# Second expert layer: block sums and statistics on other engines, the activation of later pairs after a reload

## The chip, the cores and the metric

One core of one Trainium2 chip runs the whole program in one launch. The metric is device time in microseconds (us) of that launch, the median of several runs. The engines are PE (TensorE, matrix products; PEld are its weight loads), DVE (VectorE), ACT (ScalarE), POOL (GpSimd) and SP (SyncE, which here issues DMAs). Each runs its own instructions in the order in which they were issued; between engines semaphores make them wait.

## The reference

```python
def reference(**kwargs):                      # cut
    attn_out = _attn_ref(**attn_kwargs)       # 4 batches, 12 heads, 448 tokens, heads mixed before and after the softmax
    x = attn_out.transpose(0, 2, 1, 3).reshape(1792, 768)
    x = _moe_ref(x=x, **moe_kwargs)           # 768 -> 2048 -> 768, a gated activation between
    return _moe2_ref(x=x, **moe2_kwargs)

def _moe2_ref(x, w_in, w_out, g_ln):          # 768 -> 1024 -> 768
    h = x @ w_in
    e = np.exp(h - np.max(h, axis=-1, keepdims=True))
    sm = e / (np.sum(e, axis=-1, keepdims=True) + 1e-09)
    solu = h * sm
    mu = np.mean(solu, axis=-1, keepdims=True)
    var = np.mean((solu - mu) ** 2, axis=-1, keepdims=True)
    ln = (solu - mu) / np.sqrt(var + 1e-06) * g_ln
    return ln @ w_out
```

The change is in `_moe2_ref`, the second expert layer.

## The kernel before

The program has four stages, one after the other: attention, the first expert layer, and the two matrix products of the second expert layer, here called **phase 1** (`h = x @ w_in`) and **phase 2** (`ln @ w_out`). All products keep float32 precision by splitting each operand into a rounded part and a rest: three matmuls stand for one (lines 1167 to 1169).

In the second layer the 1792 tokens are 14 tiles `t` of 128, worked on as 7 **pairs** `p`. For each pair the 2 by 2 blocks of the left matrix (two tiles of tokens by two halves of the inner dimension) and of the weights are multiplied in seven block products instead of eight (`SEVEN`; `product` and `keep_` in `seven`). Such a scheme needs sums of blocks on the left, S1 to S4 (`s_sum`, line 1086, in phase 1; `l_sum`, line 1121, in phase 2), sums of weight blocks (`prep1`, `prep2`, lines 948 to 951), and additions of the products (`part_copy` on ACT, line 1181; `part_add` on DVE, line 1184). Some products may start only when an earlier addition has released or filled their PSUM bank.

Phase 1 works through one pair like this. The left blocks and sums are split by ACT (`x2_h`, line 1092) and DVE (`x2_l`, line 1095). PE makes seven products of 9 matmuls. ACT and DVE collect them into two tiles `h` of 128x1024. For each tile DVE takes the maximum (`h2_max`, 1235), ACT the exponential with its sum (`h2_exp`, 1239), POOL and DVE make the reciprocal (1242, 1245), DVE multiplies `h`, `e` and the reciprocal in place over `e` (`h2_solu`, 1248), and SP stores the result to a DRAM scratch `xl2` (`h2_store`, 1253). For pairs below `EARLY` (2) the layer norm's mean and variance are made at once (`stat`, 1141 and 1142, on DVE; `rstd`, 1146 to 1148, on POOL).

Phase 2 loads a tile back (`el_load`, 1103), makes the statistics of pairs from `EARLY` on, normalizes on ACT (`el_ln`, 1152), transposes on PE (`tr`, 1108), copies from PSUM (`lf_copy`, 1115), makes the block sums (1121), splits (`l_h` on ACT, 1132; `l_l` on DVE, 1135) and makes seven products of 12 matmuls. While phase 1 ends, the 28 pieces of `w_out` are loaded (`w_load`, 1044) into the buffers that the last products of phase 1 leave, and split (`w_h` on ACT, 1047; `w_l`, 1051, odd pieces on POOL, even ones on DVE).

Buffers: `h2` has 5 tiles, `wout` (which holds `e`) 3, `s` (block sums) 4, `ot` (outputs) 3. The order of every engine's instructions is made when the program is built: `Order` takes tasks with a duration and a priority given in the code (`add(engine, duration, priority, function, ...)`, smaller goes first) and lists them in a simulated time; the engines then run them in that order. A changed engine or duration can thus move the instructions around it.

Of the kernel before, what the change touches and what calls it, by code (L numbers as in the profile page):

```python
# [7 lines left out]
F32 = mybir.dt.float32  # L8
# [649 lines left out]
def moe(nc, od, pl, c1, c2, last_x, r_sr, r_psa, r_psb, near, xs, c_near, c_in2, c_out2, c_t1, c_t2, c_o2, xl2, w_in, w_out, w_in2, w_out2, g_ln, ident_in, out):  # L658
    add = od.add
# [7 lines left out]
    def open1():  # L667
        pl.open([(n, b, 'right', SB) for n, b in (('wout', 3), ('win', 3), ('t', 2), ('raw', 2), ('m', 2), ('v', 1))])
        keep['half'] = pl['v'].tile([128, 1], F32, tag="half", name="half")
        keep['ebias'] = pl['v'].tile([128, 1], F32, tag="ebias", name="ebias")  # L670
        nc.gpsimd.memset(keep['half'], 0.5)
        nc.gpsimd.memset(keep['ebias'], -896.0 * 2**23)
# [332 lines left out]
    def close_o():  # L1005
        pl.close(['g', 'psb'])
        pl.open([('h2', 5, 'left', SB), ('st2', 3, 'left', SB), ('st3', 4, 'left', SB), ('pw', 4, 'left', PSUM)])
# [10 lines left out]
    ring.update({n: od.ring(b) for n, b in dict(st3=4, s=4, ot=3, h2=5, pstr=4).items()})  # L1018
# [55 lines left out]
    sx, ht, et, st, lnp, ott, elt, lf = ({} for _ in range(8))  # L1074
# [23 lines left out]
    EL = ('h2', 'h2', 'h2', 'wout')  # L1098

    def el_load(t):  # L1100
        n = EL[t % 4]
        elt[t] = pl[n].tile([128, 1536 if n == 'wout' else FF2], F32, tag=n, name="el")[:, :FF2]
        nc.sync.dma_start(out=elt[t], in_=xl2[:, t])

    def tr(t, i):
        ps = pl['pstr'].tile([128, 4, 128], F32, tag="pstr", name="ps_tr")
        for j in range(4):
            nc.tensor.transpose(ps[:, j], elt[t][:, i * 512 + j * 128:i * 512 + (j + 1) * 128], keep['ident'])  # L1108
        lnp[t, i] = ps
# [27 lines left out]
    def stat(t, late):  # L1137
        if late:
            st[t] = pl['st3'].tile([128, 32], F32, tag="st3", name="st3")
# [4 lines left out]
    def rstd(t):  # L1144
        s, r = st.pop(t), keep['ls'][:, 2 * t:2 * t + 2]
        nc.gpsimd.tensor_scalar(s[:, 6:7], s[:, 5:6], 1e-6, 1.0, op0=ALU.add, op1=ALU.mult)
        nc.gpsimd.tensor_tensor(out=r[:, 0:1], in0=s[:, 6:7], in1=keep['mh'], op=ALU.pow)
        nc.gpsimd.tensor_scalar(r[:, 1:2], s[:, 4:5], r[:, 0:1], -1.0, op0=ALU.mult, op1=ALU.mult)
# [21 lines left out]

    def out_tile(ph, t):
        d = ht if ph == 0 else ott
        if t not in d:
            d[t] = pl[('h2', 'ot')[ph]].tile([128, (FF2, DM)[ph]], F32, tag=('h2', 'ot')[ph], name=('h2', 'ot')[ph])
        return d[t].rearrange("p (i n) -> p i n", i=2)
# [10 lines left out]
    def seven(ph, p, pr, ldeps, wdeps, r_left):  # L1186
        n = (512, 384)[ph]
        mm, dur, bank, m = ring['pw'], (9 * 227, 12 * 174)[ph], {}, []
        rg = ring[('h2', 'ot')[ph]]
        own = len(rg.users)  # L1190
# [42 lines left out]
    def h2_max(t):  # L1233
        st[t] = pl['st2'].tile([128, 32], F32, tag="st2", name="st2")
        nc.vector.tensor_reduce(st[t][:, 0:1], ht[t], axis=AX.X, op=ALU.max, negate=True)  # L1235

    def h2_exp(t):
        et[t] = pl['wout'].tile([128, 1536], F32, tag="wout", name="e")[:, :FF2]
        nc.scalar.activation(out=et[t], in_=ht[t], func=AF.Exp, bias=st[t][:, 0:1], accum_out=st[t][:, 1:2])

    def h2_guard(t):
        nc.gpsimd.tensor_scalar(st[t][:, 2:3], st[t][:, 1:2], 1e-9, 1.0, op0=ALU.add, op1=ALU.mult)

    def h2_recip(t):
        nc.vector.reciprocal(st[t][:, 3:4], st[t][:, 2:3])

    def h2_solu(t):
        nc.vector.scalar_tensor_tensor(  # L1248
            out=et[t], in0=ht.pop(t), scalar=st[t][:, 3:4], in1=et[t], op0=ALU.mult, op1=ALU.mult
        )  # L1250

    def h2_store(t):
        nc.sync.dma_start(out=xl2[:, t], in_=et[t])
# [19 lines left out]
    x2_a, x2_all, ln_d, ls_d, EARLY = [], [], {}, {}, 2  # L1273
    front = {}

    def make_front(p, q0):
        for a in range(2):
            t = 2 * p + a
            x = od.dma("SP", 450, 1500, q0 - 25, el_load, t, deps=[ln_d[t]], new=[ring[EL[t % 4]]])
            ue = [(ring[EL[t % 4]], len(ring[EL[t % 4]].users) - 1)]  # L1280
            if p >= EARLY:
                us = [(ring['st3'], len(ring['st3'].users))]
                x = add("DVE", 1574, q0 - 11, stat, t, True, deps=[x], new=[ring['st3']], use=ue)
                x = add("Pool", 1055, q0 - 11, rstd, t, deps=[x], use=us)
            x = add("Activation", 1240, q0 - 11, el_ln, t, deps=[x, *ls_d[t]], use=ue)
            for i in range(2):
                m = add("PE", 436, q0 - 12 + 0.1 * (2 * a + i), tr, t, i, deps=[x], new=[ring['pstr']], use=ue)
                front[t, i] = m, [(ring['pstr'], len(ring['pstr'].users) - 1)]

    for p in range(7):  # L1290
# [22 lines left out]
        for a, (own, ds) in enumerate(seven(0, p, pr, ld, [sum((w1_d[i, k] for k in range(3)), []) for i in range(7)], r_x2)):  # L1313
            t = 2 * p + a
            uh = [(ring['h2'], own)]
            b = add("DVE", 1224, pr + a, h2_max, t, deps=ds, new=[ring['st2']], use=uh)
            us = [(ring['st2'], t)]
            b = add("Activation", 1303, pr + a, h2_exp, t, deps=[b], new=[ring['wout']], use=uh + us)
            ue = [(ring['wout'], -1)]
            b = add("Pool", 162, pr + a, h2_guard, t, deps=[b], use=us)  # L1320
            b = add("DVE", 163, pr + a, h2_recip, t, deps=[b], use=us)
            b = add("DVE", 1284, pr + a, h2_solu, t, deps=[b], use=uh + ue + us)
            ls_d[t] = []
            if p < EARLY:
# [16 lines left out]
    for p in range(7):  # L1341
# [12 lines left out]
        en, eng, dur = "Pool", nc.gpsimd, 1206  # L1354
# [27 lines left out]
def tile_kernel(ctx, tc, q, k, v, w_pre, w_post, w_in, w_out, w_in2, w_out2, g_ln, eye, mask, out):  # L1382
# [73 lines left out]
```

## Time and profile before

| | us |
|---|---|
| median of 3 runs | 1088.41 (1080.71 to 1089.03) |
| the profiled execution, its own time | 1083.43 |
| its span, first to last instruction | 1081.7 |
| PE / DVE / ACT / POOL busy | 1031.6 / 754.9 / 605.1 / 418.3 |

The span is 1.7 us less than the execution's own time. "Busy" is the time in which an engine works on an instruction; matmuls overlap in the pipeline, so a single one lasts longer than the distance to the next. "Idle before" is the time an engine stood still before an instruction, and what stands behind the arrow ended that wait.

### The profile page before, as it was taken

How to read it: one execution, taken by the hardware profiler on the slowest of the kernel's cores; microseconds unless marked ns; L12 is line 12 of the kernel's file. 1: busy time of each engine (PE TensorE's matmuls, PEld its weight loads, DVE VectorE, ACT ScalarE, POOL GpSimd, SP SyncE). 2: the span in 40 equal slices, each digit the busy share in tenths (PEclk: the TensorE clock that was granted, in tenths of full speed). 3: DMA queues.
4: the chain of work that ended last, by engine and by line, in shares of the span. 5: the costliest groups of instructions: out<-in, count | busy, mean ns of one | idle time of the engine just before them, and what ended most of it. 6: DMA issues, size and time to landing. Idle time of an engine off the chain costs nothing. (4 is left out here: it accounts for less than half of the span.)

```text
span 1081.7 us, 27329 instructions
## 1 busy us (share of the span) xinstructions
PE 1031.6 (95%) x11053; PEld 842.8 (78%) x11053; DVE 754.9 (70%) x1235; ACT 605.1 (56%) x1301; POOL 418.3 (39%) x513
## 2 busy tenths in 40 slices
PE   6889997999998999999999999999999999989998
PEld 2445665756655799999999999999989787779998
DVE  4555564655556853587878677897876999998653
ACT  3777786887877665443433334343345455677531
POOL 3121222111111433354544455554511668276432
PEclk8899999999999999999999999999999999999999
DMA  8786777586748441323323243333274454574111
GB/s 179 218 212 189 228 218 204 150 230 175 207 140 280 128 136 43 112 80 117 117 89 116 68 129 120 118 131 117 88 245 141 169 190 153 177 278 151 64 59 59
DMA packets 99119, 163.02 MB, mean 151 GB/s; under 512 B 22497, under 2 KB 77633, under 8 KB 98993
## 3 DMA queue, kind: packets, MB, share of 16 engines
q1 hardware_dynamic: 98256, 160.07, 48.0%
q0 software_dynamic: 736, 1.21, 0.6%
q8 instruction: 87, 1.43, 0.6%
q14 instruction: 40, 0.32, 0.1%
HBM read 86.88 MB, written 35.65 MB: 113 GB/s over the span
## 5 line engine op out<-in xcount | busy, mean ns | idle before, releaser
L851 PE MATMUL ps_o<-g,wout 128*128 128x448 f32 x384 | 140.5, 366 | 0.8 <-DVE x2acc L861 0.8
L853 PE MATMUL ps_o<-g,wout 128*128 128x448 f32 x384 | 140.5, 366 | 0.0
L852 PE MATMUL ps_o<-g,wout 128*128 128x448 f32 x384 | 140.5, 366 | 0.0
L345 DVE TENSOR_REDUCE nm<-ps_pre 128x1 f32<-128x448 f32 x180 | 105.7, 617 | 48.7 <-PE ps_pre L340 43.6
L376 PEld LDWEIGHTS ps_post<-wr,p 64*64 64x64 f32 x5040 | 104.3, 136 | 44.6 <-issue 28.9
L350 ACT ACTIVATE p<-ps_pre,nm 128x448 f32<-128x448 f32 x180 | 114.5, 644 | 25.6 <-DVE nm L345 24.8
L843 POOL TENSOR_TENSOR g<-t,g 128x448 fp32r<-128x448 f32 x64 | 82.6, 1292 | 114.2 <-ACT g L839 113.1
L861 DVE TENSOR_TENSOR x2acc<-ps_o,x2acc 128x448 f32<-128x448 f32 x168 | 100.7, 616 | 23.9 <-PE ps_o L853 22.1
L740 POOL TENSOR_TENSOR m<-m,v 128x768 f32<-128x768 f32 (+1 forms) x48 | 88.7, 1847 | 73.2 <-DVE v L722 56.2
L313 PE MATMUL ps_qk<-kraw,qb 64*64 64x448 f32 (+2 forms) x768 | 106.4, 586 | 10.1 <-DMA qb<-in_q_dram 4.4
L376 PE MATMUL ps_post<-wr,p 64*64 64x60 f32 x5040 | 104.3, 221 | 9.7 <-issue 6.7
L340 PE MATMUL ps_pre<-sr,wp 64*64 64x448 f32 (+1 forms) x720 | 103.9, 578 | 8.5 <-DMA qb<-in_q_dram 3.3
L324 ACT ACTIVATE s<-ps_qk 119x448 f32<-119x448 f32 (+1 forms) x186 | 92.0, 570 | 29.8 <-PE ps_qk L313 19.1
L357 POOL TENSOR_SCALAR nm<-nm 128x2 f32<-128x2 f32 x90 | 19.8, 220 | 225.5 <-ACT p L350 225.3
L827 ACT ACTIVATE t<-ps_h,half 128x448 f32<-128x448 f32 x64 | 40.4, 631 | 76.9 <-PE ps_h L823 75.6
L851 PEld LDWEIGHTS ps_o<-g,wout 128*128 128x128 f32 x384 | 72.1, 188 | 7.3 <-DVE x2acc L861 1.2
L712 ACT ACTIVATE v<-v,ebias 128x768 int32<-128x768 int32 (+1 forms) x48 | 42.2, 879 | 63.3 <-DVE v L708 63.3
L852 PEld LDWEIGHTS ps_o<-g,wout 128*128 128x128 f32 x384 | 72.1, 188 | 6.2
L853 PEld LDWEIGHTS ps_o<-g,wout 128*128 128x128 f32 x384 | 72.1, 188 | 6.1
L340 PEld LDWEIGHTS ps_pre<-sr,wp 64*64 64x64 f32 (+1 forms) x720 | 31.0, 137 | 53.1 <-issue 16.5
L427 PE MATMUL ps_av<-at,vv 128*64 128x240 f32 (+1 forms) x648 | 69.2, 354 | 2.4 <-issue 2.3
L821 PE MATMUL ps_h<-sr,win 128*128 128x448 f32 x192 | 70.9, 369 | 0.0
(190 smaller groups left out, 2504.5 us busy)
## 6 DMA issues: line engine op xcount, KB each, us to landing
sr<-s SPq DMA_DIRECT2D x138, 192.5 KB
raw<-in_moe_w_out_dram SPq DMA_DIRECT2D x22, 768.0 KB
raw<-in_moe_w_in_dram SPq DMA_DIRECT2D x14, 768.0 KB
sr<-s SPq DMA_DIRECT2D x48, 210.0 KB
xl<-e SPq DMA_DIRECT2D x14, 512.0 KB
el<-xl SPq DMA_DIRECT2D x14, 512.0 KB
raw<-in_moe_w_in_dram SPq DMA_DIRECT2D x12, 512.0 KB
kraw<-in_k_dram SPq DMA_DIRECT2D x24, 224.0 KB
```

What stands on the lines that cost most here:

```text
L313: nc.tensor.matmul(out=qk_t[b, c, 2 * p + e][64 * j:at_], lhsT=qb[rows, i % 2, lo:hi], rhs=kraw_t[b, p][rows], start=True, stop=True,)
L324: nc.scalar.activation(out=s[:n], in_=qk_t.pop((b, c, h))[:n], func=AF.Copy, scale=0.125)
L340: nc.tensor.matmul(out=pre_t[t][o:o + 64], lhsT=wp[k_], rhs=sr[i % 2][k_, g, :], start=True, stop=True)
L345: nc.vector.tensor_reduce(nm_t[t // 2][:, 0, t % 2:t % 2 + 1], pre_t[t], axis=AX.X, op=ALU.max, negate=True)
L350: nc.scalar.activation(out=p, in_=pre_t.pop(t), func=AF.Exp, bias=nm[:, 0, e], accum_out=nm[:, 1, e])
L376: nc.tensor.matmul(out=ps[i][64 * j:64 * j + 64, k, :], lhsT=ps_p[e][64 * i:64 * i + 64, x:x + 64], rhs=wr[64 * i:64 * i + 64, e], start=T ...
L740: nc.gpsimd.tensor_tensor(out=m, in0=m, in1=vt.pop(key).bitcast(F32)[:, :n], op=ALU.mult)
L843: nc.gpsimd.tensor_tensor(out=g[:, 1], in0=tt.pop((u, j)), in1=f(g[:, 0]), op=ALU.subtract)
L851: nc.tensor.matmul(out=ps, lhsT=wh, rhs=g[:, 0], start=(i == 0), stop=False)
L852: nc.tensor.matmul(out=ps, lhsT=wh, rhs=g[:, 1], start=False, stop=False)
L853: nc.tensor.matmul(out=ps, lhsT=wl, rhs=g[:, 0], start=False, stop=(i == 1))
L861: nc.vector.tensor_tensor(out=dst, in0=op.pop((u, m)), in1=dst, op=ALU.add)
```

## The change

The block sums of both phases go from POOL to DVE. The statistics are no longer made by `stat`: the multiplication of `h2_solu` also gives its sum, POOL makes the negative mean of it, ACT squares the tile with that mean as bias and gives the sum of squares (its output overwrites `h`), and POOL makes the factor and the shift. `EARLY` becomes 3. For pairs 3 to 6 phase 1 stores both `e` and `h` right after the exponential, and the steps from the reciprocal to the statistics run in phase 2 after both are loaded. Small tiles (statistics, two constants) go into one tile of a new pool opened ahead of `wout`; `st2`, `st3` and `ls` fall away.

```diff
-        pl.open([(n, b, 'right', SB) for n, b in (('wout', 3), ('win', 3), ('t', 2), ('raw', 2), ('m', 2), ('v', 1))])
+        pl.open([(n, b, 'right', SB) for n, b in (('pad', 1), ('wout', 3), ('win', 3), ('t', 2), ('raw', 2), ('m', 2), ('v', 1))])
+        t = pl['pad'].tile([128, 272], F32, name="st")
+        keep['st'], keep['half'], keep['ebias'] = t[:, :8 * NT // 128].rearrange("p (t i) -> p t i", i=8), t[:, 112:113], t[:, 113:114]
...
-EL = ('h2', 'h2', 'h2', 'wout')
-    def el_load(t):
-        n = EL[t % 4]
+    def el_load(t, what):
+        n = 'wout' if t >= 2 * EARLY and not what else 'h2'
...
+        nc.sync.dma_start(out=d, in_=(xe2, xh2)[what][:, t])
...
-    def stat(t, late):
-        for i in range(2):
-            nc.vector.bn_stats(out=st[t][:, 8 + 6 * i:14 + 6 * i], in_=(elt if late else et)[t][:, 512 * i:512 * i + 512])
-        nc.vector.bn_aggr(out=st[t][:, 4:6], in_=st[t][:, 8:20])
...
+    def h2_solu(t):
+        nc.vector.scalar_tensor_tensor(
+            out=et[t], in0=ht[t], scalar=sc(t, 3), in1=et[t], op0=ALU.mult, op1=ALU.mult, accum_out=sc(t, 4)
+        )
+
+    def h2_mean(t):
+        nc.gpsimd.tensor_scalar(sc(t, 5), sc(t, 4), -1.0 / FF2, 0.0, op0=ALU.mult, op1=ALU.add)
+
+    def h2_square(t):
+        nc.scalar.activation(out=ht[t], in_=et[t], func=AF.Square, bias=sc(t, 5), accum_out=sc(t, 6))
+
+    def h2_rstd(t):
+        nc.gpsimd.tensor_scalar(sc(t, 6), sc(t, 6), 1.0 / FF2, 1e-6, op0=ALU.mult, op1=ALU.add)
+        nc.gpsimd.tensor_tensor(out=sc(t, 6), in0=sc(t, 6), in1=keep['mh'], op=ALU.pow)
+        nc.gpsimd.tensor_tensor(out=sc(t, 7), in0=sc(t, 5), in1=sc(t, 6), op=ALU.mult)
+
+    def solu(t, pr, deps, ue, uh):
+        x = add("Pool", 250, pr, h2_guard, t, deps=deps)
+        x = add("DVE", 163, pr, h2_recip, t, deps=[x])
+        y = add("DVE", 1360, pr, h2_solu, t, deps=[x], use=uh + ue)
+        x = add("Pool", 250, pr, h2_mean, t, deps=[y])
+        x = add("Activation", 1330, pr, h2_square, t, deps=[x], use=uh + ue)
+        return y, add("Pool", 1300, pr, h2_rstd, t, deps=[x])
...
-EARLY = ... 2
+EARLY = ... 3
...
             if p >= EARLY:
-                x = add("DVE", 1574, q0 - 11, stat, t, True, deps=[x], new=[ring['st3']], use=ue)
-            x = add("Pool", 1055, q0 - 11, rstd, t, deps=[x], use=us)
+                y = od.dma("SP", 450, 1500, q0 - 25, el_load, t, 1, deps=[lh_d[t]], new=[ring['h2']])
+                _, x = solu(t, q0 - 11, [x, y, ls_d[t]], ue, uh)
...
-            en, eng, dur = ("Pool", nc.gpsimd, 930) if p else ("DVE", nc.vector, 465)      # s_sum
+            en, eng, dur = "DVE", nc.vector, 550
...
             if p < EARLY:
+                b, ls_d[t] = solu(t, pr + a, [b], ue, uh)
+            else:
+                lh_d[t] = od.dma("SP", 450, 1500, pr + a, h2_store, t, 1, deps=[b], use=uh)
+                ls_d[t] = b
+            ln_d[t] = od.dma("SP", 450, 1500, pr + a, h2_store, t, 0, deps=[b], use=ue)
...
-        en, eng, dur = "Pool", nc.gpsimd, 1206                                              # l_sum
+        en, eng, dur = "DVE", nc.vector, 675
```

## Rows read from the trace of the kernel before

**Rows 1.** Windows by stage: length, busy us of PE, PEld, DVE, ACT, POOL (instructions), granted PE clock, DMA share, GB/s.
```profile
845.40:972.00 126.60, 116.33 (x514) 94.53 (x513) 121.88 (x166) 73.29 (x137) 80.69 (x85) 0.99 0.54 188
860.30:875.00 14.70, 14.70 (x65) 12.00 (x65) 13.63 (x22) 7.71 (x15) 8.12 (x14) 1.00 0.61 221
905.00:926.00 21.00, 18.53 (x79) 14.54 (x79) 21.00 (x28) 12.04 (x25) 14.37 (x14) 1.00 0.44 153
943.00:960.30 17.30, 16.08 (x76) 13.45 (x74) 16.79 (x22) 13.32 (x28) 14.47 (x12) 1.00 0.99 348
960.30:972.00 11.70, 7.95 (x37) 7.07 (x37) 11.70 (x16) 9.04 (x17) 7.60 (x8) 0.85 0.52 172
972.00:1078.00 106.00, 105.35 (x628) 103.88 (x628) 65.74 (x102) 50.88 (x86) 44.27 (x51) 1.00 0.24 86
```

**Rows 2.** Timeline of PE, its waits after 845 us: start, duration, form, [idle before <-releaser].
```profile
855.85 0.50 PE L1167 MATMUL ps_h<-xl,x 128*128 128x512 f32 x1 [2.08 <-DVE h L1184]
898.67 0.50 PE L1169 MATMUL ps_h<-sr,x 128*128 128x512 f32 x1 [0.67 <-DVE x L1095]
915.97 0.50 PE L1167 MATMUL ps_h<-xl,x 128*128 128x512 f32 x1 [0.53 <-DVE h L1184]
920.27 0.47 PE L1167 MATMUL ps_h<-xl,x 128*128 128x512 f32 x1 [1.94 <-DVE st L1245]
956.71 0.50 PE L1167 MATMUL ps_h<-xl,x 128*128 128x512 f32 x1 [1.22 <-DVE h L1184]
966.97 0.69 PE L1167 MATMUL ps_ot<-sr,acc 128*128 128x384 f32 x1 [3.46 <-ACT ot L1181]
```

**Rows 3.** Groups of DVE from 845 to 971 us: form, count | busy us, mean ns | idle before.
```profile
L1095 DVE TENSOR_TENSOR x<-s,x 128x384 fp32r<-128x384 f32 x26 | 20.3, 792 | 0.0
L1248 DVE SCALAR_TENSOR_TENSOR e<-h,st,e 128x1024 f32<-128x1024 f32 x14 | 20.2, 1450 | 0.2
L1235 DVE TENSOR_REDUCE st<-h 128x1 f32<-128x1024 f32 x14 | 16.8, 1202 | 0.0
L1095 DVE TENSOR_TENSOR x<-x2acc,x 128x384 fp32r<-128x384 f32 x19 | 16.2, 854 | 0.4 <-ACT x L1092 0.4
L1141 DVE BATCH_NORM_STATS2 st<-e 128x6 f32<-128x512 f32 x8 | 5.1, 680 | 0.0
```

**Rows 4.** Single lines, whole run: count, duration ns min/median/max, first and last start.
```profile
L1095 DVE TENSOR_TENSOR x<-s,x x28: 541/553/1373, 841.3 to 943.0; 128x384 fp32r<-128x384 f32 x28
L1086 DVE TENSOR_TENSOR s<-x2acc x2: 547/548/548, 836.4 to 838.8; 128x384 f32<-128x384 f32 x2
L1086 POOL TENSOR_TENSOR s<-x2acc x12: 1018/1240/1992, 841.9 to 924.7; 128x384 f32<-128x384 f32 x12
L1248 DVE SCALAR_TENSOR_TENSOR e<-h,st,e x14: 1268/1283/2033, 868.0 to 968.0; 128x1024 f32<-128x1024 f32 x14
L1121 POOL TENSOR_TENSOR lf<-lf x28: 1283/1300/1951, 946.6 to 1065.5; 128x512 f32<-128x512 f32 x28
L1135 DVE TENSOR_TENSOR acc<-lf,acc x12: 692/1310/1775, 949.9 to 1066.4; 128x512 fp32r<-128x512 f32 x12
L1239 ACT ACTIVATION_READ_ACCUMULATOR e<-h,st x14: 183/186/192, 863.8 to 964.7; 128x1 f32 x14
```

**Rows 5.** Timelines of DVE and ACT where phase 1 ends.
```profile
968.05 2.03 DVE L1248 SCALAR_TENSOR_TENSOR e<-h,st,e 128x1024 f32<-128x1024 f32 x1
...
961.27 1.15 ACT L1239 ACTIVATE e<-h,st 128x1024 f32<-128x1024 f32 x1 [2.63 <-DVE st L1235]
...
964.80 1.75 ACT L1047 ACTIVATE xl<-xl 128x384 fp32r<-128x384 f32 x4
966.45 0.47 ACT L1181 ACTIVATE ot<-ps_ot 128x384 f32<-128x384 f32 x1
```

**Rows 6.** Windows around the last loads of phase 2's weights, columns as in rows 1.
```profile
962.00:964.00 2.00, 1.51 (x8) 0.90 (x6) 2.00 (x4) 2.00 (x6) 1.18 (x3) 1.00 0.05 19
...
974.00:978.00 4.00, 4.00 (x27) 3.96 (x25) 3.97 (x9) 2.22 (x3) 1.96 (x6) 1.00 1.00 395
```

More of the change, by code (lines that the diff above doesn't have):

```diff
@@ L1006, in close_o @@
         pl.close(['g', 'psb'])
-        pl.open([('h2', 5, 'left', SB), ('st2', 3, 'left', SB), ('st3', 4, 'left', SB), ('pw', 4, 'left', PSUM)])
+        pl.open([('h2', 5, 'left', SB), ('pw', 4, 'left', PSUM)])
     def reuse_a():
@@ L1072, in moe @@
             w1_d[i, k] = w_piece(w1_at(i, k), 512, src, 1290 + 2 * i + 0.1 * k, deps + [ch_ if q == 4 else o2], **kw)
[L1074 removed]
+    sx, ht, et, lnp, ott, lf = ({} for _ in range(6))
     def block(p, a, k):
@@ L1095, in x2_l @@
         nc.vector.tensor_tensor(out=x2v(i, 1), in0=left(p, q), in1=f(x2v(i, 0)), op=ALU.subtract)
-    EL = ('h2', 'h2', 'h2', 'wout')
-    def el_load(t):
-        n = EL[t % 4]
-        elt[t] = pl[n].tile([128, 1536 if n == 'wout' else FF2], F32, tag=n, name="el")[:, :FF2]
-        nc.sync.dma_start(out=elt[t], in_=xl2[:, t])
+    def el_load(t, what):
+        n = 'wout' if t >= 2 * EARLY and not what else 'h2'
+        d = pl[n].tile([128, 1536 if n == 'wout' else FF2], F32, tag=n, name=("el", "hl")[what])[:, :FF2]
+        (et, ht)[what][t] = d
+        nc.sync.dma_start(out=d, in_=(xe2, xh2)[what][:, t])
     def tr(t, i):
@@ L1135, in l_l, with sc @@
         nc.vector.tensor_tensor(out=lt(p, i)[:, 1], in0=l_src(p, q), in1=f(lt(p, i)[:, 0]), op=ALU.subtract)
-    def stat(t, late):
-        if late:
-            st[t] = pl['st3'].tile([128, 32], F32, tag="st3", name="st3")
-        for i in range(2):
-            nc.vector.bn_stats(out=st[t][:, 8 + 6 * i:14 + 6 * i], in_=(elt if late else et)[t][:, 512 * i:512 * i + 512])
-        nc.vector.bn_aggr(out=st[t][:, 4:6], in_=st[t][:, 8:20])
[L1144 to L1148, printed above, removed]
+    def sc(t, i):
+        return keep['st'][:, t, i:i + 1]
@@ new lines, in h2_guard, with h2_recip @@
+    def h2_guard(t):
+        nc.gpsimd.tensor_scalar(sc(t, 2), sc(t, 1), 1e-9, 1.0, op0=ALU.add, op1=ALU.mult)
+    def h2_recip(t):
+        nc.vector.reciprocal(sc(t, 3), sc(t, 2))
+    def h2_solu(t):
[6 more added lines that the diff above has]
+        nc.scalar.activation(out=ht[t], in_=et[t], func=AF.Square, bias=sc(t, 5), accum_out=sc(t, 6))
@@ L1169, in wide_mm, with out_ring @@
             nc.tensor.matmul(out=ps, lhsT=ll, rhs=w[:, 0], start=False, stop=z, skip_group_check=True)
+    def out_ring(ph, t):
+        return ('h2', 'ot')[ph]
     def out_tile(ph, t):
-        d = ht if ph == 0 else ott
+        d, n = (ht, ott)[ph], out_ring(ph, t)
         if t not in d:
-            d[t] = pl[('h2', 'ot')[ph]].tile([128, (FF2, DM)[ph]], F32, tag=('h2', 'ot')[ph], name=('h2', 'ot')[ph])
+            d[t] = pl[n].tile([128, dict(h2=FF2, ot=DM, wout=1536)[n]], F32, tag=n, name=('h2', 'ot')[ph])[:, :(FF2, DM)[ph]]
         return d[t].rearrange("p (i n) -> p i n", i=2)
@@ L1188, in seven @@
         mm, dur, bank, m = ring['pw'], (9 * 227, 12 * 174)[ph], {}, []
-        rg = ring[('h2', 'ot')[ph]]
-        own = len(rg.users)
+        rgs = {str(a + 1): ring[out_ring(ph, 2 * p + a)] for a in range(2)}
         first_out = {}
@@ L1233, in h2_max, with h2_store @@
     def h2_max(t):
-        st[t] = pl['st2'].tile([128, 32], F32, tag="st2", name="st2")
-        nc.vector.tensor_reduce(st[t][:, 0:1], ht[t], axis=AX.X, op=ALU.max, negate=True)
+        nc.vector.tensor_reduce(sc(t, 0), ht[t], axis=AX.X, op=ALU.max, negate=True)
     def h2_exp(t):
         et[t] = pl['wout'].tile([128, 1536], F32, tag="wout", name="e")[:, :FF2]
[L1239 to L1253, printed above, removed]
+        nc.scalar.activation(out=et[t], in_=ht[t], func=AF.Exp, bias=sc(t, 0), accum_out=sc(t, 1))
+    def h2_store(t, what):
+        nc.sync.dma_start(out=(xe2, xh2)[what][:, t], in_=(et, ht)[what][t])
     def store(t, c0, n):
@@ L1393, in tile_kernel @@
     c_o2 = dram.tile([128, 4, 2, DM], F32, name="c_o2")
-    xl2 = dram.tile([128, NT // 128, FF2], F32, name="xl2")
+    xe2 = dram.tile([128, NT // 128, FF2], F32, name="xe2")
+    xh2 = dram.tile([128, NT // 128, FF2], F32, name="xh2")
     with tc.manual_schedule():
         c1, c2, last_x, r_sr, r_psa, r_psb, near = attention(nc, od, pl, q, k, v, w_pre, w_post, mask, xs, w_in, w_out, c_near)
-        moe(nc, od, pl, c1, c2, last_x, r_sr, r_psa, r_psb, near, xs, c_near, c_in2, c_out2, c_t1, c_t2, c_o2, xl2, w_in, w_out, w_in2, w_out2, g_ln, eye, out)
+        moe(nc, od, pl, c1, c2, last_x, r_sr, r_psa, r_psb, near, xs, c_near, c_in2, c_out2, c_t1, c_t2, c_o2, xe2, xh2, w_in, w_out, w_in2, w_out2, g_ln, eye, out)
         od.emit()
```

41 lines of the change are left out of this document (15 added, 26 removed).

## The prediction

> **What bounds the kernel now.** I read the windows by stage first, for they say whether the second layer has anything to gain, then PE's timeline for its waits there, then the groups of VectorE for what stands in front of the instructions that PE waits for. The profiled execution took 1083.43 us, its span 1081.7; the three timed runs have their median at 1088.41, 5 us above it, and spread over 8.3 us. About 1% (11 us) is what a measurement of this kernel can tell from no change.
>
> The change works from 845 us on: phase 1 to about 960, phase 2 to 1078. In phase 2, from 972 on, PE is busy 105.35 of 106.00 us [rows 1]: nothing that makes VectorE, ScalarE or GpSimd faster there can shorten it, it can only stay as full. From 845.4 to 972 VectorE is busy 121.88 of 126.60 us and PE has the gaps: the pair from 860.3 to 875 runs without one, the stretch from 905 to 926 leaves PE 2.5 us idle with VectorE at 21.00 of 21.00 [rows 1]. PE's waits over 0.5 us there are six, 2.08, 0.67, 0.53, 1.94, 1.22 and 3.46 us, 9.9 in all; the first five end with a VectorE instruction (an addition, a split, or the reciprocal that stands ahead of one), the sixth with ScalarE's copy of phase 2's first product [rows 2]. After the sixth the granted clock is low: 0.85 over the 11.7 us from 960.3 to 972 [rows 1], which costs 0.15 x 11.7 = 1.8 us. So the most that the change can give back is 9.9 + 1.8 = 11.7 us, 1.1%. Attention and the first expert layer, three quarters of the time, keep their instructions; only the places of some of their buffers move.
>
> **Part by part.** *Block sums of phase 1 on VectorE.* Off GpSimd go 24 instructions of up to 1.24 us (the median of the twelve that read the accumulators), onto VectorE come 24 of 0.548 us [rows 4] = +13.2 us. Against it stands what GpSimd's work does to VectorE: the split of a block sum takes 0.541 us at best and 1.373 at worst [rows 4], and 26 and 19 of the splits average 0.792 and 0.854 us [rows 3], so 36.8 us in place of 45 x 0.545 = 24.5: 12.3 us too much. GpSimd's sums are up to 24 x 1.24 = 30 of its 80.69 busy us there [rows 1, 4]; the weight sums and half of the weight splits stay on it. Their part of the 12.3 us is between their share of the time, 30/80.69 (4.6 us), and all of it; the short statistics on GpSimd can hardly count, so I take 6.
>
> *Statistics.* For the four early tiles the two passes of 0.680 us each [rows 3] go: 4 x 1.36 = 5.4 us off VectorE in phase 1. For it the multiplication gives a sum. The trace has no such instruction on VectorE. From below: free, as part of the pass. From above: a pass of its own, as the maximum over the same 1024 elements, 1.202 us [rows 3]. The nearest row is ScalarE's exponential with a sum, which is followed by a read of the accumulator of 0.186 us [rows 4]; I take that: 6 x 0.19 = 1.1 us in phase 1. The squares go to ScalarE (73.29 busy of 126.60 [rows 1]), six of about the exponential's 1.15 us [rows 5] and a read, 8 us: hidden in its idle 53, and if that cover were gone they would stand ahead of its copies. GpSimd's small steps gain room, since its 30 us of sums are gone.
>
> [...]
>
> *The multiplication of pairs 3 to 6 in phase 2.* Eight leave phase 1, at the mean of 1.450 us [rows 3] 11.6 us, among them the one of 2.03 us at 968 [rows 5]. In their stead SP issues eight more stores of 128x1024 float32, 0.52 MB each, and eight more loads in phase 2. Both stores of a tile now wait for the exponential only. Behind a waiting store on SP's queue stand the loads of phase 2's weights, but the exponential is earlier than the multiplication was, so SP waits less than before.
>
> *Sum for VectorE in phase 1*: +13.2 + 1.1 - 6 - 5.4 - 11.6 = -8.7 us, that is 113 in place of 122 of 126.6. With bounds of 0 and 7.2 for the accumulators and of 4.6 and 12.3 for the slowing it lies between -16 and -1: lighter in each case, most in pairs 3 to 6 and hardly in pair 2, which now has the sums and keeps its multiplication.
>
> *What PE gets of it.* The waits at 898.67, 915.97 and 920.27, 3.1 us, fall where VectorE is full and where pair 3's multiplications and GpSimd's sums go: I give back 2.8. The one at 855.85 (2.08) comes while VectorE splits the last weights of phase 1 beside GpSimd's weight sums, which stay; the sums of pair 1 (4 x 0.548 = 2.2 us) now enter the same queue, in front of the addition or behind it as the builder's simulated time has it. Between a gain of 2 and a loss of 2.2: 0. The one at 956.71 (1.22) stands behind splits of phase 2 of 1.310 us beside GpSimd's sums, where 0.692 is possible [rows 4], but four sums of about that length come onto VectorE too: 0.6 back. The sixth (3.46) ends with ScalarE's copy at 966.45, behind four weight splits that start at 964.80 and the exponentials; the first of these, at 961.27, had waited for VectorE's maximum [rows 5], and that needs the last products of phase 1. Its end can come little earlier: 0.5 back. The multiplication of 2.03 us at 968.05 stood ahead of the next additions [rows 5], and with a shorter wait the clock falls less: 0.6 back. Phase 1 and the passage together: 2.8 + 0 + 0.6 + 0.5 + 0.6 = 4.5 us.
>
> *Phase 2.* VectorE had 65.74 of 106 us [rows 1]. Off: the statistics of nine tiles, 9 x 1.36 = 12.2, and the slowing of splits beside GpSimd's sums (12 x (1.310 - 0.692) = 7.4 [rows 4], those into other buffers not counted). On: 24 of the 28 sums at 0.69 = 16.6, eight multiplications with a sum, 8 x 1.47 = 11.8. That makes some 75 of 106, with a pass of its own for each sum 83: still cover. ScalarE gets eight squares, 50.88 + 8 x 1.34 = 62. The chain of a tile grows by the multiplication and the square, 2.8 us, with the short steps between them and one more load, against 106 / 7 = 15 us that a pair gives. Cost 0; if an addition is caught behind a multiplication now and then, up to 1.
>
> Sum: 1083.43 - 4.5 = 1078.9 for an execution like the profiled one, 1088.41 - 4.5 = 1083.9 at the median's level. I name the middle, 1081.
>
> **The rivals.** *The full DMA takes VectorE's place.* From 943 to 960.3 the DMA engines are busy 0.99 at 348 GB/s, with phase 2's weights in the queue [rows 1]. The two `h` stores of pair 5 go in just ahead: 1.05 MB / 348 GB/s = 3.0 us. Against it: the DMA is nearly still from 962 to 964 (0.05 [rows 6]) and the last splits start at 964.80 [rows 5], so up to 3 us of lateness is covered. From 974 to 978 it is full again at 1.00 with the reloads [rows 6], and pair 6's `h` adds 1.05 MB / 395 GB/s = 2.7 us. This decides if the last weight pieces land after ScalarE reaches their splits. If both delays reach PE and the clock stays low for as long again (1.8), it costs 7.5 against 4.5 gained: 1086.4, or 1091 at the median's level, slower than before.
>
> *The passage opens.* With a new order the copy at 966.45 is put ahead of the exponentials (its product was made before the last ones of phase 1), and the wait of 3.46 us and the low clock go: a further 4 us, 8.5 to 11 us in all, 1073 or 1078. For it: nothing but the order holds the copy. Against: the last weight pieces' splits end only after 966 [rows 5], so PE would soon wait for these.
>
> *Each sum costs a pass of its own*: 6 x 1.202 [rows 3] = 7.2 us more in pairs 0 to 2, of which VectorE fills 13.63 of 14.70 us [rows 1]. Pair 2, which gets no relief, would fall behind by its two, 2.4 us, and pair 1 by some tenths: 1.5 us of gain stay: 1082, or 1087. [...]
>
> *It doesn't do what it says*: VectorE drops by 8.7 us but PE's waits only move, since the order's simulated durations differ from the real ones: 1083, or 1088.
>
> **How the numbers follow.** Forecast 0.45, full DMA 0.15, open passage 0.2, passes for the sums 0.1, waits that only move 0.1. From 1073 less the spread of runs to 1091: 1071 to 1091 at the level between profiled run and median. Faster by over 1% needs nearly the whole ceiling: 0.17, most of the open passage. Slower by over 1% needs the DMA's delays and more: 0.05. Within 1%: 0.78.
>
> **What the profile after would show.** GpSimd's busy time down by some 60 us; splits of block sums near 0.55 us; the multiplication with its sum as one instruction of 1.28 us and a short read, or of 2.5; PE without waits from 895 to 925, the wait at phase 2's start still over 2 us; phase 2 as full as before. Wrong would make it: a new wait of PE in phase 2, or weights that land after 965.

## The result and the profile after

Over 20 executions of each, the changed kernel's median is 1076.79 us (1068.51 to 1087.62) against 1091.65 (1080.71 to 1101.09): 14.9 us or 1.4% less, and a ratio of 0.9856 with an interval of 0.9825 to 0.9887. Here and below the medians count all executions, the ratios only those within 1.5% of the fastest of their kernel (16 and 19 of these 20). The prediction was 1081 us with a gain of 4.5. The profiled execution took 1078.25 us, its span 1076.4.

Single executions scatter by 20 us, so I compare the stages inside a trace. The limits are starts of matmuls in TensorE's timeline; here are those of the changed kernel: the first of the first expert layer, the last of that layer, the last of phase 1 and the last of phase 2.

```profile
372.30 0.47 PE L820 MATMUL ps_h<-sr,win 128*128 128x448 f32 x1
...
843.64 0.36 PE L852 MATMUL ps_o<-g,wout 128*128 128x448 f32 x1
...
950.63 0.40 PE L1186 MATMUL ps_h<-w1x,x 128*128 128x512 f32 x1
...
1072.59 0.34 PE L1186 MATMUL ps_ot<-xl,x 128*128 128x384 f32 x1
```

The first layer takes 843.64 - 372.30 = 471.3 us, phase 1 (with the step into it) 107.0, the rest 122.0. The same subtraction for all profiled executions (names as in the experiments below; us):

```
kernel         up to layer 1  layer 1  phase 1  rest   layer 2  both layers
before             364.5       480.7    113.5   119.1   232.6    713.3
control            359.7       479.9    116.6   119.1   235.7    715.6
before_pad         377.0       475.1    115.2   118.9   234.1    709.3
after_nopad        358.5       481.8    106.6   122.3   228.9    710.7
nopad_r16          362.8       475.4    107.0   123.0   230.0    705.4
pad256             371.7       485.8    105.7   121.2   226.8    712.6
after              372.3       471.3    107.0   122.0   228.9    700.3
after_again        370.2       471.4    107.4   122.5   229.9    701.2
early7             376.4       471.6    107.9   123.3   231.2    702.8
accum_only         375.7       471.8    111.5   122.1   233.6    705.4
ssum_pool          363.3       471.5    109.8   122.3   232.0    703.5
ln_late            361.1       472.1    106.8   114.8   221.6    693.6
ln_late_again      369.7       471.6    107.2   114.8   222.0    693.6
front_early        364.9       471.1    107.3   113.2   220.5    691.6
```

So the gain has two sources. Layer 1 falls from 480.8 (mean of before, control and after_nopad, which have the old places of the buffers) to 471.4 (after and after_again): 9.4 us. Layer 2 falls from 234.1 (the three with the old layer 2) to 228.9 (the five with the new one: after, after_again and the three of other places): 5.2 us. Together 14.6 of the measured 14.9. The stage before layer 1 lies anywhere between 358 and 377 us, at two values 8.6 us apart for one and the same kernel, and is not compared.

Layer 1 in the windows view of before: busy us and (in brackets) the instructions of PE, weight loads, DVE, ACT and POOL, then the granted clock, the DMA's share and GB/s.

```profile
600.00:800.00 200.00, 200.00 (x983) 184.28 (x982) 160.65 (x225) 77.14 (x118) 98.83 (x70) 1.00 0.38 123
```

And of after:

```profile
600.00:800.00 200.00, 200.00 (x1001) 187.46 (x1001) 162.49 (x230) 78.16 (x120) 102.63 (x72) 1.00 0.37 123
```

PE is full and at its full clock in both, and still 1001 matmuls fit where 983 did: 199.8 ns from one to the next in place of 203.5. Times the layer's 2304 matmuls that is 8.5 us of the 9.4; some 0.6 more is after_nopad's, whose layer 1 has 3.4 us at a granted clock of 0.50 near its start (363.5 to 366.9). PE's idle time before these matmuls is under 1 us in both (0.8 and 0.3), so the gain is no wait that went: the same matmuls follow one another faster.

Layer 2, in answer to [rows 1], by windows of after:

```profile
843.80:970.20 126.40, 120.56 (x560) 100.75 (x558) 108.86 (x174) 82.55 (x152) 46.70 (x62) 0.99 0.68 242
970.20:1072.70 102.50, 100.38 (x584) 98.21 (x584) 66.75 (x118) 57.48 (x99) 14.66 (x38) 0.98 0.31 104
...
960.00:964.00 4.00, 4.00 (x27) 3.97 (x26) 1.27 (x3) 0.04 (x1) 1.20 (x3) 1.00 1.03 345
964.00:968.00 4.00, 1.40 (x13) 1.16 (x11) 0.94 (x2) 0.67 (x2) 0.00 (x0) 1.00 0.94 343
968.00:972.00 4.00, 1.81 (x5) 1.58 (x6) 1.38 (x2) 4.00 (x7) 0.00 (x0) 0.55 0.99 404
972.00:976.00 4.00, 4.00 (x19) 3.90 (x19) 3.65 (x7) 1.56 (x5) 0.57 (x1) 0.60 0.06 25
```

PE's waits of after, in answer to [rows 2]: us in total, times, longest.

```profile
PE ps_ot L1184 <- ACT xl L1130: 4.8, 1, 4.8
PE ps_h L1184 <- DVE h L1204: 1.1, 1, 1.1
PE ps_ot L1186 <- DVE acc L1133: 0.8, 1, 0.8
PE ps_ot L1184 <- DVE ot L1204: 0.7, 1, 0.7
PE ps_ot L1184 <- ACT ot L1201: 0.6, 1, 0.6
```

Of the five waits of phase 1 one of 1.1 us is left (at 855.55). At the passage into phase 2 the old wait of 3.46 us is gone, and a new one of 4.8 stands there with all engines nearly idle (964 to 968) except the DMA, and with the granted clock at 0.55 and 0.60 in the 8 us from 968 on. It fell while PE stood still (1.00 from 966 to 968.4, 0.50 from 968.4 on) and stayed at 0.50 until 975.2; PE was at work for 5 us of that time:

```profile
968.40:975.20 6.80, 5.01 (x17) 4.69 (x18) 4.46 (x8) 4.36 (x9) 0.38 (x1) 0.50 0.56 229
```

DVE's groups of after from 843.8 to 970.2, in answer to [rows 3]: form, count | busy us, mean ns | idle before.

```profile
L1254 DVE TENSOR_REDUCE st<-h 128x1 f32<-128x1024 f32 x14 | 16.9, 1210 | 0.0
L1094 DVE TENSOR_TENSOR x<-s,x 128x384 fp32r<-128x384 f32 x26 | 14.9, 579 | 0.0
L1094 DVE TENSOR_TENSOR x<-x2acc,x 128x384 fp32r<-128x384 f32 x19 | 13.3, 701 | 1.3 <-ACT x L1091 1.3
L1145 DVE SCALAR_TENSOR_TENSOR e<-h,st,e 128x1024 f32<-128x1024 f32 x6 | 8.2, 1364 | 0.0
...
L1085 DVE TENSOR_TENSOR s<-x2acc 128x384 f32<-128x384 f32 x12 | 6.6, 551 | 0.0
...
L1085 DVE TENSOR_TENSOR s<-x2acc,s 128x384 f32<-128x384 f32 x6 | 3.7, 617 | 0.0
L1085 DVE TENSOR_TENSOR s<-s,x2acc 128x384 f32<-128x384 f32 x6 | 3.3, 553 | 0.1
```

The instruction that [rows 4] lacked, by line, over the whole run: count, ns min/median/max, first and last start.

```profile
L1145 DVE SCALAR_TENSOR_TENSOR e<-h,st,e x6: 1269/1272/1821, 865.6 to 899.1; 128x1024 f32<-128x1024 f32 x6
L1145 DVE DVE_READ_ACCUMULATOR e<-h,st,e x6: 72/76/80, 866.8 to 900.3; 128x1 f32 x6
```

### The profile page after: what moved, and what is told of

It is laid out like the page before. It is cut to its first block, busy times and chain, and to the rows that moved or that the text cites. A ratio compares the mean times of both kernels' runs of the same rounds, so it can differ in the third digit from the quotient of the medians.

```text
span 1076.4 us, 27349 instructions
## 1 busy us (share of the span) xinstructions
PE 1026.5 (95%) x11053; PEld 840.0 (78%) x11053; DVE 741.8 (69%) x1259; ACT 621.6 (58%) x1329; POOL 352.5 (33%) x475
## 4 chain that ended last, share of the span: by engine, by line
PE 77%; DMA 11%; DVE 5%; ACT 4%; issue 2%; POOL 1%; SPq 1%; ACTq 0%; DVEq 0%
PE ps_h L820 7%; PE ps_o L850 7%; PE ps_h L822 7%; PE ps_o L852 7%; PE ps_h L821 7%; PE ps_o L851 7%; DMA sr<-s 5%; PE ps_pre L340 5%; PE ps_av L427 5%; PE ps_post L376 4%; PE ps_qk L313 4%; PE ps_h L1184 3%; PE ps_h L1186 3%; PE ps_h L1185 3%; PE ps_ot L1186 3%; PE ps_ot L1184 3%
## 5 line engine op out<-in xcount | busy, mean ns | idle before, releaser
L850 PE MATMUL ps_o<-g,wout 128*128 128x448 f32 x384 | 139.4, 363 | 0.3 <-DVE x2acc L860 0.3
L852 PE MATMUL ps_o<-g,wout 128*128 128x448 f32 x384 | 139.2, 363 | 0.0
L851 PE MATMUL ps_o<-g,wout 128*128 128x448 f32 x384 | 138.3, 360 | 0.0
L313 PE MATMUL ps_qk<-kraw,qb 64*64 64x448 f32 (+2 forms) x768 | 110.2, 593 | 12.5 <-DMA qb<-in_q_dram 5.1
L826 ACT ACTIVATE t<-ps_h,st 128x448 f32<-128x448 f32 x64 | 40.3, 630 | 69.1 <-PE ps_h L822 67.7
L711 ACT ACTIVATE v<-v,st 128x768 int32<-128x768 int32 (+1 forms) x48 | 42.2, 880 | 64.3 <-DVE v L707 64.1
```

Of the source, the lines that this page charges most:

```text
L313: nc.tensor.matmul(out=qk_t[b, c, 2 * p + e][64 * j:at_], lhsT=qb[rows, i % 2, lo:hi], rhs=kraw_t[b, p][rows], start=True, stop=True,)
L850: nc.tensor.matmul(out=ps, lhsT=wh, rhs=g[:, 0], start=(i == 0), stop=False)
L851: nc.tensor.matmul(out=ps, lhsT=wh, rhs=g[:, 1], start=False, stop=False)
L852: nc.tensor.matmul(out=ps, lhsT=wl, rhs=g[:, 0], start=False, stop=(i == 1))
```

## Experiments

In the expectations, layer 1 is counted from the 7500th matmul, some 7 to 8.5 us after its first, so its figures there are that much below the table's.

**What the places of the buffers do.** control is the kernel before, once more.

> The kernel before, unchanged, for a second profile on the chip on which the next three run. Theory placement (the first expert layer is faster because its right-hand buffers lie 1088 bytes lower): its matmuls start every 0.2039 us here too, as in the first profile of the kernel before, so that 250 of them take 51.0 us. Rival chip (the two profiles compared so far came from different executions or chips, and the step belongs to these): a step near 0.2000 us is as likely here.

It took 1080.94 us; its row and that of before show how far two traces of one kernel differ: 0.8 us in layer 1, 3.1 in layer 2. The 3.1 are about what the clock costs, by an estimate from its figures: after its waits of 2.1 and 1.9 us, which before has as well, control shows 0.50 from 851.6 to 855.0 and 0.51 from 916.5 to 919.9, where before stayed at 1.00; two stretches of 3.4 us at 0.50 are 3.4 us of work by that figure. The theory of the places holds and the chip falls as a cause: control fits 983 matmuls into 600 to 800 us, like before, and early7, run on the same chip with the changed kernel's places, 1002.

before_pad is the kernel before with the right-hand buffers of layer 1 moved down by 1088 bytes by a new tile, into which its small statistics tiles are laid; engines and order stay:

```diff
-        pl.open([(n, b, 'right', SB) for n, b in (('wout', 3), ('win', 3), ...
+        pl.open([(n, b, 'right', SB) for n, b in (('pad', 1), ('wout', 3), ('win', 3), ...
+        keep['pad'] = pl['pad'].tile([128, 272], F32, name="pad")
...
```

> The kernel before with the pool of 272 floats opened ahead of wout and its statistics tiles laid into it, nothing else. Theory placement: step of the first expert layer's matmuls 0.200 us, 2304 x 0.0039 = 9 us less, ratio 0.992. Rival chip: step as in the control, ratio 1.000. Rival left side (the 128 bytes that the removed tile moves xl and g): 1.000 too, since the left side stays.

Layer 1 took 475.1 us, 5.7 less where the theory had 9, with 993 matmuls in the same window; layer 2 stayed at 234.1. Timed, the ratio is 0.998 (0.9942 to 1.0018): the 5.7 us lie inside that interval, but the timing alone does not show them.

after_nopad is the changed kernel with every buffer of layer 1 at its old place (`st` on the left, behind `h2`, the constants and `ls` where they were).

> The changed kernel with every buffer of the first expert layer at its old address (no pool ahead of wout, the statistics in a pool behind h2, a dummy tile in the place of ls). Theory placement: step 0.2039 us, only the 3.6 us of the second layer stay, ratio 0.996. Rival chip: ratio 0.986 as the changed kernel. Rival left side: 0.996 as well; the kernel with the right side alone moved tells the two apart.

Layer 1 went back to 481.8 us, with 983 matmuls in the window, and layer 2 stayed at 228.9. Timed 0.9899 (0.9854 to 0.9944), medians 1083.85 against 1089.28. The ratio's interval overlaps that of the changed kernel, so the timing alone does not part the two; the stages do, by 10 us in layer 1. So layer 1's gain hangs on the places, and layer 2's does not.

nopad_r16 has an unused pool of 16 floats (64 bytes) ahead of `wout` in after_nopad; pad256 is the changed kernel with 256 floats in `st` in place of 272. The first moves the right side by 64 bytes, the second by 1024.

> The changed kernel with its small tiles back on the left (as in after_nopad), and the right-hand buffers of the first expert layer 64 bytes lower by an unused pool of 16 floats. after_nopad had a median matmul step of 203 to 204 ns in the first expert layer and 473.3 us for that layer; the changed kernel, 1088 bytes lower, had 200 to 201 ns and 464.4 us. If what counts is the place of the buffers within 1024 bytes (1088 is 1024 and 64), the step is 200 to 201 ns here too and the layer takes 464 to 468 us. If the 1 KB shift counts, step and layer stay at 203 to 204 ns and 471 to 475 us. Second layer: 229 us either way.

> The changed kernel with its pool of small tiles of 256 floats instead of 272, so that the right-hand buffers of the first expert layer lie 1024 bytes lower than in the kernel before instead of 1088. If the place within 1024 bytes counts, the step goes back to 203 to 204 ns and the first expert layer to 471 to 475 us; if any shift of about 1 KB does it, the step stays at 200 to 201 ns and the layer at 464 to 468 us. The left side is that of the changed kernel in both cases. Second layer: 229 us either way.

nopad_r16, windows:

```profile
600.00:800.00 200.00, 199.73 (x990) 185.37 (x989) 160.62 (x229) 78.78 (x121) 98.05 (x69) 1.00 0.39 126
```

pad256, windows:

```profile
600.00:800.00 200.00, 200.00 (x969) 181.63 (x969) 160.13 (x216) 77.79 (x119) 100.78 (x72) 1.00 0.33 109
```

With the left side at its old place, 64 bytes give 475.4 us, about all that 1088 bytes gave in before_pad. 1024 bytes with the left side of after, where `g` and `xl` lie 128 bytes lower, give a loss of 5 us: 206.4 ns for a matmul and 485.8 us. So the rule that I named, the place of the right side within 1024 bytes, fails: by it pad256 was to come out at 203 ns. The left side counts too: after has 200 ns where before_pad, with the same right side, has 201.4. It is not the whole of the rest. `sr` lies at one place in all these kernels, and `win` in pad256 exactly 1024 bytes below its place in before. Of 36 products of these two in a row, the first and the last start 7.09 us apart in before and 7.23 in pad256; of the eight such groups of each, before has seven between 7.09 and 7.11 and one of 7.23, pad256 all at 7.23. PE's timeline, before:

```profile
602.20 0.36 PE L821 MATMUL ps_h<-sr,win 128*128 128x448 f32 x1
...
609.29 0.36 PE L823 MATMUL ps_h<-sr,win 128*128 128x448 f32 x1
```

And pad256:

```profile
612.22 0.37 PE L820 MATMUL ps_h<-sr,win 128*128 128x448 f32 x1
...
619.45 0.37 PE L822 MATMUL ps_h<-sr,win 128*128 128x448 f32 x1
```

That the places make the difference is shown; by what rule, and which buffer meets which, is open.

**What each part is worth in layer 2.** early7 leaves the activation of all pairs in phase 1 (`EARLY` is 7 in place of 3), so no `h` is stored or loaded again.

> The changed kernel with EARLY = 7: all pairs are activated in phase 1, nothing of h is stored or reloaded. Theory full DMA (the wait of 4.8 us at the start of phase 2 and the low clock behind it come from the h stores and loads): the wait falls under 1 us and with it the low clock, 6 us less; VectorE in phase 1 gains 8 x 1.36 = 11 us and stays under 120 of 126, so phase 1 gets 0 to 3 us of waits; 3 to 6 us faster than the changed kernel, ratio to before 0.981 to 0.983. Rival (moving the activation out of phase 1 is what freed PE): waits of 4 us or more come back in phase 1, ratio 0.986 or more.

Phase 1 took 107.9 us, layer 2 231.2, 1.8 over the mean of the two runs of the changed kernel; timed 0.9942 (0.9911 to 0.9973), medians 1082.16 against 1089.28, 7 us of the 10 to 13 that its stages show. The DMA's wait at the passage is gone, and a longer one stands there, behind VectorE. So the theory failed, for the wait did not fall under 1 us but rose to 6.5; and of the rival only the ratio came true, for in phase 1 no wait over 1.0 us came back. early7, windows:

```profile
955.00:960.00 5.00, 3.98 (x23) 3.48 (x21) 5.00 (x7) 3.23 (x8) 5.00 (x5) 1.00 0.97 365
960.00:965.00 5.00, 0.00 (x0) 0.00 (x0) 4.92 (x7) 5.00 (x12) 4.27 (x8) 0.65 0.61 207
965.00:970.00 5.00, 3.61 (x10) 3.10 (x11) 5.00 (x6) 2.20 (x6) 4.96 (x4) 0.50 0.28 112
```

early7, PE's waits from 945 to 975:

```profile
PE ps_ot L1185 <- DVE sr L1050: 7.4, 2, 6.5
```

VectorE is full for 15 us with the last multiplications and phase 2's weight splits side by side. Moving the activation out keeps it free there (2.2 of 8.0 us busy in after from 960 to 968), at the price of a full DMA (1.03 and 0.94).

ssum_pool puts the block sums of pairs 1 to 6 in phase 1 back on POOL:

```diff
-            en, eng, dur = "DVE", nc.vector, 550
+            en, eng, dur = ("Pool", nc.gpsimd, 930) if p else ("DVE", nc.vector, 465)
```

> The changed kernel with the block sums of pairs 1 to 6 in phase 1 back on POOL (sums of phase 2 stay on VectorE). My theory after the first runs: moving the activation of pairs 3 to 6 out of phase 1 is what removed TensorE's waits there, and the place of the sums is worth little: VectorE gets 24 x 0.57 = 13.6 us back but its splits are slowed again by some 8 us; phase 1 stays at 106 to 108 us and the second layer at 228 to 231 us. Rival: the sums on POOL, at 1.2 us each and behind the guards and powers of the normalization, hold back the splits of x: phase 1 gets 3 to 7 us longer (110 to 114 us) and the second layer 232 to 236 us.

Phase 1 took 109.8 us (105.7 to 107.4 in the five with the sums on VectorE), layer 2 232.0. My theory had the place of the sums worth little; in this one execution it is worth 2 to 3 us, just at the low end of the rival. ssum_pool, DVE's groups:

```profile
L1094 DVE TENSOR_TENSOR x<-s,x 128x384 fp32r<-128x384 f32 x26 | 19.2, 737 | 2.0 <-ACT x L1091 2.0
```

ssum_pool, PE's waits up to 945 us:

```profile
PE ps_h L1184 <- DVE h L1204: 3.3, 2, 2.1
```

The same 26 splits rise from 579 to 737 ns, and PE waits 3.3 us for additions where it had waited 1.1. VectorE's busy time is no larger for it (107.15 of 126.00 us, against 108.86 of 126.40 in after). So a split of one form takes 158 ns more with the sums on POOL, while POOL's other work stays in both; by what mechanism is not shown.

accum_only was to leave the accumulators alone of all parts, but as built only phase 2's sums went back to POOL, with `EARLY` at 7; phase 1's sums stayed on VectorE. It leaves out less of the change than its expectation says.

> The changed kernel with all block sums back on POOL and the activation of all pairs in phase 1: of the change's parts in the second layer only the statistics by accumulators are left. The kernel before took 232.6 and 235.7 us for the second layer in two executions. If the accumulators are worth what their rows say (2 x 0.68 us of bn_stats per tile less one read of 0.08, some 5 us of VectorE in phase 1), VectorE ends at 115 to 118 us busy in phase 1, the waits there shrink, and the layer takes 231 to 234 us. Rival: the mean and the square, now on POOL and ScalarE one after the other, queue behind POOL's sums and hold back the stores and loads of pair 0 and 1, and the layer takes 234 to 238 us.

It took 1086.8 us in its one execution, phase 1 111.5, layer 2 233.6. Read as early7 with phase 2's sums on POOL, it puts some 2.4 us on these sums, by one execution of each. What the accumulators alone are worth was not run.

No part carries the gain of phase 1 by itself: with one or two undone it still takes 107.9 to 111.5 us against 113.5 to 116.6 before, and two traces of one kernel differ by up to 3 us in layer 2, so the single shares (moved activation 2, phase 1's sums 3, phase 2's sums 2) are sizes, not figures.

**The passage.** What after's PE waits for at 970.19, by the chain of waits from 950 to 975 us (start, us, what):

```profile
954.69 7.06 DMA xh<-h
961.74 0.02 issue
961.76 0.03 SPq L1101
961.79 0.03 issue
961.82 5.96 DMA el<-xe
...
967.93 1.24 ACT el L1169
969.17 0.48 ACT lf L1113
969.65 0.50 ACT xl L1130
970.15 0.04 issue
970.19 0.69 PE ps_ot L1184
```

And ACT's timeline of after there:

```profile
944.86 0.49 ACT L1201 ACTIVATE ot<-ps_ot 128x384 f32<-128x384 f32 x1 [0.99 <-PE ps_ot L1186]
...
964.56 0.60 ACT L1130 ACTIVATE x<-ps_tr 128x512 fp32r<-128x512 f32 x1 [4.52 <-PE ps_tr L1106]
967.93 1.24 ACT L1169 ACTIVATE el<-el,st 128x1024 f32<-128x1024 f32 x1 [2.77 <-DMA el<-xe]
969.08 0.58 ACT L1113 ACTIVATE lf<-ps_tr 128x512 f32<-128x512 f32 x1
969.55 0.59 ACT L1130 ACTIVATE xl<-ps_tr 128x512 fp32r<-128x512 f32 x1
```

A new `h` store takes 7.06 us of a full DMA; the buffer that it empties is the one into which SP then loads one of pair 2's tiles, 5.96 us more; ScalarE, in order, stands before that tile's normalization, and pair 1's copies and halves, which PE needs now, queue behind it though their input is there (PE's transposes end at 965.40, the first of these copies starts at 969.08). ln_late changes this order alone: `late` holds two high halves of pair 1.

```diff
-            x = add("Activation", 1240, q0 - 11, el_ln, t, deps=[x, ls_d[t]], use=ue)
+            x = add("Activation", 1240, q0 - 11, el_ln, t, deps=[x, ls_d[t], *late], use=ue)
...
-            make_front(p, pr)
+            make_front(p, pr, l0 if p == 2 else ())
...
             ld.append([x, y])
+        l0 = [ld[0][0], ld[2][0]]
```

> The changed kernel with one more order on ScalarE: the normalization of pair 2's two tiles is issued after the first high halves of pair 1, so that a late load of its activation does not hold them back. My theory: TensorE's 4.8 us wait at the passage into phase 2 is ScalarE standing 2.8 us in front of that load, with pair 1's copies and halves queued behind it; the wait shrinks to 1 to 2.5 us, the lower clock after it shortens, and the second layer takes 224 to 227 us instead of 229.0. Rival: the DMA queue is the bound there, and whatever stands in its place waits for another load (pair 2's transposes, or the weights): the wait returns within 20 us behind it and the second layer stays at 228 to 231 us.

> The same kernel as ln_late, timed in rounds. Its second layer took 221.6 us in the first look against 229.0 in the changed kernel, where the wait at the passage had shrunk from 4.8 to 0.8 us and the stretch behind it kept the full clock. If that is no accident of one execution, the second layer takes 221 to 223 us again, and the time is 6 to 9 us below that of the changed kernel and 18 to 24 us below the kernel before (ratio 0.978 to 0.984). Rival: the landing of that load varies from run to run and the wait comes back in part: 224 to 229 us, ratio 0.983 to 0.990.

> The changed kernel once more, unchanged, as the base for ln_late_again on the same chip: ratio 0.983 to 0.989 to the kernel before, first expert layer 464 to 465 us, second layer 228 to 230 us. If its second layer or its first layer fell outside these by over 2 us, the stage times of single profiles would be less sure than I take them to be.

Layer 2 took 221.6 and 222.0 us. Timed side by side, ln_late_again has 0.9823 (0.9781 to 0.9865), median 1069.48, and after_again 0.9841 (0.9791 to 0.9892), median 1076.01, with the kernel before at 1088.47. The intervals overlap, so timing alone does not part the two; the stages do, by 7 to 8 us in each trace. ln_late_again, windows:

```profile
960.00:964.00 4.00, 3.31 (x26) 3.04 (x24) 1.33 (x3) 1.52 (x4) 0.00 (x0) 1.00 0.99 311
964.00:968.00 4.00, 3.79 (x22) 3.29 (x23) 2.22 (x5) 4.00 (x8) 0.00 (x0) 1.00 1.02 410
968.00:972.00 4.00, 4.00 (x26) 3.74 (x26) 4.00 (x7) 4.00 (x8) 1.09 (x2) 1.00 0.83 296
```

ln_late_again, PE's waits there:

```profile
PE ps_ot L1184 <- ACT xl L1130: 0.8, 1, 0.8
```

The DMA is as full as before, so the rival (the DMA as the bound) falls. The wait shrinks by 4.0 us and the clock stays at 1.00; in after, 5.01 us of PE's work at 0.50 are 2.5 us lost by that figure, and 2.3 by the distance of its matmuls of 384 columns (0.32 us there, 0.17 at 1.00 from 976 on). With the wait of 0.8 us behind `acc` in phase 2, which ln_late has no more, that is 4.0 + 2.5 + 0.8 = 7.3, the whole difference of the two traces; my forecast of 224 to 227 had left a wait of 1 to 2.5 us and part of the low clock standing.

front_early is ln_late with `make_front(p, pr - 9, ...)` for pair 1, so that its first transposes stand among pair 0's products.

> ln_late, and in addition the transposes of pair 1 are given an earlier place in TensorE's order, two of the four groups among pair 0's products instead of all behind them. Theory: what is left of the wait at the passage (0.8 us, and some 0.5 us of slow steps) goes too, and the second layer takes 220 to 221.5 us. Rival: the transposes now stand in TensorE's queue before their input or their bank of PSUM is free, and the products behind them wait: 222 to 226 us.

One execution took 1062.15 us, layer 2 220.5; PE has no wait over 0.5 us at the passage, with the DMA's share at 0.98 to 1.04 from 948 to 964. It is the shortest pair of layers of all (691.6 us), 1 to 2 us below ln_late, which one execution cannot settle.

## Why the prediction was right in part, and where it was not

The time lies in the range, but the gain is 14.9 us where the sum had 4.5, and its likeliest class, within 1%, was missed: 1.4% faster, to which 0.17 was given. That the time lies in the range is in good part luck: most of the gain comes from a stage that the forecast left as it was. That layer 2's 5.2 us are near the 4.5 is luck too: phase 1 gave 5.0 more than forecast and the passage 4.3 less.

**The step that failed** is "Attention and the first expert layer, three quarters of the time, keep their instructions; only the places of some of their buffers move", costed at nothing. It is the largest term: 9.4 of 14.6 us. The places change the length of a matmul (after_nopad, nopad_r16, pad256), so a term per matmul times 2304 was due, between a loss of some 5 us (pad256) and a gain of 9. No row of before showed a second place; its sign could not be had from the trace, but the bound could not be nought.

**VectorE in phase 1** was forecast at 113 of 126.6 us and is 108.86 of 126.40. Term by term: block sums +13.6 (forecast +13.2); accumulator reads 6 x 0.076 = +0.5 (+1.1); the slowing, 45 splits at 28.2 us where [rows 3] have 36.5, -8.3 (-6, bounds 4.6 to 12.3); statistics -5.1 (-5.4); the multiplications 20.2 to 8.2, -12.0 (-11.6). The slowing was the one mis-sized by over 1 us; the value lay inside the bounds, and nearer their middle. These terms make -11.3 of the -13.0; the rest is many small groups, among them the weight splits (-0.8).

**The sum as one pass.** 1.272 us with a sum against 1.283 without, and a read of 0.076. The rival of a pass of its own falls.

**What PE gets of it.** In phase 1 the four later waits [rows 2] went, the three from 898 to 920 and the one at 956 in full, and the one at 855.85 fell from 2.08 to 1.05 us at 855.55; phase 1 became 8.4 us shorter by the means of the table (115.1 to 106.7), 6.5 between these two traces, where the forecast had 3.4. Some 1.6 of the 8.4 are what control and before_pad take over before's own 113.5 (3.1 and 1.7 us). In control the lower clock behind the old waits makes it up by the estimate above (0.50 and 0.51, where before had 1.00); that it does so in before_pad is not shown. The changed kernel's trace is at 1.00 through phase 1 (843.8 to 951). "Between a gain of 2 and a loss of 2.2: 0" was a gain of 1.

**The passage** was to give 1.1 us and cost 3.2 (119.0 to 122.2 in the table's rest). Two rivals came true at once. It opened: ScalarE's copy, at 966.45 in [rows 5], now stands at 944.86. And the full DMA took its place, yet not by the way that I named: not phase 2's weights landed late, but a reload of the activation. "SP waits less than before" looked at the queue alone; the moved multiplication also leaves `h` in its buffer until the store has landed, and the next load into that ring waits for it. The price that I worked out, 7.5 us, is near the 4.8 + 2.5 that it cost, but from other terms.

**Phase 2** stays covered, as forecast: VectorE 66.75 of 102.5 us (forecast 75 of 106), ScalarE 57.48 (62), three waits of 0.6 to 0.8, 2.0 together (cost 0 to 1; the one at the end, 0.65, before had too). GpSimd's busy time fell from 418.3 to 352.5 us (some 60 forecast).

## What to carry to other kernels

A change that allocates a tile ahead of the operands of a bound TensorE stage can change that stage (here from a loss of 5 us to a gain of 9): put the new tile where nothing moves, or try a few places on purpose, and compare the matmuls per window before crediting the edit. Moving work off an engine also moves the life of its buffers: look at which load takes the buffer next, not only at the queue. And before calling a passage bound by the DMA, see what stands behind the waiting instruction on its in-order engine: one more edge in the order gave back 7 us under the same DMA load.

## What was not expected of the hardware

One instruction stream, a full PE and a granted clock of 1.00, and yet 199.8, 201.4, 203.5 or 206.4 ns from one 448-column fp32r matmul to the next (1001, 993, 983 and 969 in 200 us), by the places of the layer's buffers in SBUF; 64 bytes were enough for some 2 ns (nopad_r16 has 993 from 400 to 600 us, after_nopad 983). Why is open: no run here changes what the other engines do in layer 1. In PE's wait of 4.8 us the granted clock fell to 0.50 and stayed there until 975.2, 5.0 us after PE's work began again, while the wait of 1.1 us in phase 1 left it at 1.00 (852 to 860). A wait of 2.1 us went either way: 1.00 behind it in before (852 to 862), 0.50 in control (851.6 to 855.0).
